# Low-rank mixing of an attention + mixer kernel: full sums of 32 rows and four row tiles at once, in two visits

## The chip, the cores and the metric

The kernel runs on one core of one Trainium2 chip. The metric is the device time of one execution in microseconds (us). Engines are named as the profile names them: PE (TensorE matmul), PEld (its weight load), DVE (VectorE), ACT (ScalarE), POOL (GpSimd), SP (SyncE, which issues most DMA). "Batch" is the index b from 0 to 7. Runs of one group were made on one chip beside runs of the kernel before on that chip; a ratio is the mean time of one kernel's fast runs over the mean of the other's fast runs of the same rounds, so it is not quite the ratio of the medians quoted beside it.

## The reference, cut to what matters

```python
# attention with RMS-normed q and k, 8 batches, 12 heads, 448 tokens, head size 64 -> x (8, 448, 768)
h   = x.transpose(0, 2, 1) @ U @ V          # low-rank token mixing: U 448x32, V 32x448
u   = x + h.transpose(0, 2, 1)
out = u + relu(u @ w_ch1) @ w_ch2           # channel MLP, 768 -> 3072 -> 768
```

In the layout of the kernel (tokens in partitions) the mixing of a batch is t = U^T x (32 x 768) and then u = x + V^T t. Tokens lie in four tiles of 128 rows.

## The kernel before

The main loop runs the MLP of batch b as a generator of short runs of matmuls. Between these runs it weaves first the attention of batch b+1 and then the mixing of batch b+1. The numbers `FA` and `FM` say which share of the MLP the attention and the mixing are spread over. Batch 0 is mixed otherwise and is not touched.

```python
FA, FM, NPE, FA0 = (0.74, 0.77), 0.09, 14, 0.66
...
def mix_t(b):                       # four partial sums, one per token tile, in four row groups of 32
    pm = ps_s.tile([P, 2, 512], FP32, tag="s", name="pm")
    for half in range(2):
        for i in range(4):
            nc.tensor.matmul(pm[i * rank:(i + 1) * rank, half, 0:HALF], Ub[:, b % 2, i, :],
                             xt[i][:, half * HALF:(half + 1) * HALF], start=True, stop=True)
    nc.scalar.activation(t4b.rearrange("p (h n) -> p h n", h=2), pm[:, :, 0:HALF], AF.Copy)

def mix_u(b, i, halves=(0, 1)):     # V stands four times in V4, so K=128 also adds the four partial sums
    pu = ps_s.tile([P, 2, 512], FP32, tag="s", name="pu") if b else ...
    for k, half in enumerate(halves):
        nc.tensor.matmul(pu[:, k, 0:HALF], lhsT, t4s[b][:, half * HALF:(half + 1) * HALF], start=True, stop=True)
    nc.vector.tensor_add(xv, pu[rows, 0:n, 0:HALF], xv)

def mix_uT(b, i):                   # u of the next first layer, transposed by DMA
    nc.sync.dma_start_transpose(us[b][:, :, i * P:(i + 1) * P], ...)

def mixing(b):
    items = [(1, lambda: mix_t(b))]
    for i in range(4):
        items.append((1, lambda i=i: (mix_u(b, i), mix_uT(b, i))))
    return items
...
def transposes(p):                  # q and k of a head pair; by DMA from batch 2 on (NPE = 14)
    if p < NPE: ...
    else:
        nc.sync.dma_start_transpose(qkT.rearrange("d s (j p) -> d (s j) p", j=NJ), qkn)

def gains(p):                       # the gain of q, on DVE, before the scores
    if p >= NPE:
        nc.vector.tensor_scalar(qkTs[p][:, 1], qkTs[p][:, 1], gg, None, OP.mult)
```

The score and mixing products share a pool of two PSUM tiles of two banks each (`ps_s`).

## Time and profile before

| | kernel before |
|---|---|
| time, median of 3 | 580.18 us (579.93 to 580.73) |
| PE busy | 562.7 of 579.7 us |
| product with V (`pu`), batches 1 to 7 | about 1.30 us each |
| x·U (`pm`), batches 1 to 7 | 0.44 us each |

The lines below are from the page of the kernel before: the span, the busy time of each engine with its share and count of instructions, the DMA queue that brings instructions (packets, MB, share of 16 engines' span), and the shares of the chain that ended last.

```profile
span 579.7 us, 11362 instructions
...
PE 562.7 (97%) x4613; PEld 306.5 (53%) x4613; DVE 397.8 (69%) x811; ACT 280.2 (48%) x413; POOL 78.3 (14%) x122
...
q8 instruction: 36, 0.59, 0.4%
...
PE 85%; DVE 7%; DMA 3%; ACT 2%; issue 1%; POOL 1%; DVEq 0%; POOLq 0%; ACTq 0%
```

TensorE is busy nearly all the time and makes up 85% of the chain, so time taken off TensorE should show nearly in full. Note the queue of 36 packets: 2 x 4613 TensorE instructions divided by 256 is 36.

The timeline of TensorE in the mixing of batch 7, kernel before. Columns: start in us, length in us (with the pipeline's tail), engine, line, operation, tiles, shapes, count.

```profile
505.57 0.34 PE L323 MATMUL pm<-xs,Ub 128*32 128x384 bf16 x1
505.57 0.34 PE L323 MATMUL pm<-x,Ub 128*32 128x384 bf16 x3
505.74 0.33 PE L323 MATMUL pm<-xs,Ub 128*32 128x384 bf16 x1
505.75 0.33 PE L323 MATMUL pm<-x,Ub 128*32 128x384 bf16 x3
506.01 1.15 PE L413 MATMUL pb<-Tw,hT 128*128 128x384 bf16 x6
507.00 0.49 PE L337 MATMUL pu<-t4b,Vsh 128*128 128x384 bf16 x2
507.32 1.14 PE L413 MATMUL pb<-Tw,hT 128*128 128x384 bf16 x6
508.30 0.49 PE L337 MATMUL pu<-t4b,V 128*128 128x384 bf16 x2
508.62 1.14 PE L413 MATMUL pa<-w2b,hT 128*128 128x384 bf16 x6
```

Four `pm` matmuls start together (505.57) and four more at 505.74; the next product starts at 506.01, so x·U takes 0.44 us. Each `pu` pair takes 0.32 us from its start to the next product's (507.00 to 507.32), and there are four.

The groups of TensorE by form, kernel before (count, then busy us and mean ns of one, then idle time before them and who ended it), show the row-tiled scores and the two mixing products:

```profile
L273 PE MATMUL sc<-qkT 64*128 64x448 bf16 x384 | 56.1, 358 | 3.3 <-ACT E L278 1.1 <-DVE qkT L265 0.8 <-DVE qkT L259 0.6
...
L337 PE MATMUL pu<-t4b,V 128*128 128x384 bf16 x48 | 12.1, 326 | 0.0
...
L323 PE MATMUL pm<-x,Ub 128*32 128x384 bf16 x42 | 3.5, 331 | 0.0
```

And in the waits of TensorE (who waited for whom: us in total, times, longest) the score line that matters later is small:

```profile
PE sc L273 <- DVE rec L302: 0.5, 1, 0.5
```

### The profile page before, as it was taken

The page shows a single profiled execution, that of the slowest core. Times are in us where ns is not written, and L with a number is a line of the kernel's source. Part 1 is how long each engine was busy: PE and PEld are TensorE (multiplying, and loading weights), DVE is VectorE, ACT ScalarE, POOL GpSimd, SP SyncE. Part 2 cuts the span into 40 slices and gives each one's busy share as a digit, 9 for nine tenths or more (in the row PEclk, how much of TensorE's full clock was granted, in tenths as well). Part 3 has the DMA queues.
Part 4 walks back from the last instruction along what each step waited for, and adds up shares of the span by engine and source line. Part 5 has one row for each costly group of instructions (what it writes and reads, how often), then busy time and mean ns, then how long its engine had stood idle before and what let it go on. Part 6 is the DMA issues. An engine that isn't in the chain of part 4 may idle for free.

```text
span 579.7 us, 11362 instructions
## 1 busy us (share of the span) xinstructions
PE 562.7 (97%) x4613; PEld 306.5 (53%) x4613; DVE 397.8 (69%) x811; ACT 280.2 (48%) x413; POOL 78.3 (14%) x122
## 2 busy tenths in 40 slices
PE   6799999999999999999999999999999999999997
PEld 2365556544565555544466555544456555554464
DVE  5868987399875787747777498747767487453342
ACT  5856663166621876166651677236661386302200
POOL 4651421000020001000020001000002010000010
PEclk9999999999999999999999999999999999999999
DMA  9999998415563355635536354546245441040021
GB/s 217 247 241 236 216 166 188 100 49 96 112 167 91 85 115 123 149 85 112 128 82 130 82 129 113 153 111 128 60 85 163 99 97 33 29 110 0 1 55 55
DMA packets 103648, 67.22 MB, mean 116 GB/s; under 512 B 54716, under 2 KB 102060, under 8 KB 103596
## 3 DMA queue, kind: packets, MB, share of 16 engines
q1 hardware_dynamic: 93988, 56.77, 42.0%
q0 software_dynamic: 9376, 9.44, 10.0%
q8 instruction: 36, 0.59, 0.4%
q10 hardware_dynamic: 232, 0.30, 0.2%
q14 instruction: 16, 0.13, 0.1%
HBM read 52.19 MB, written 11.01 MB: 109 GB/s over the span
## 4 chain that ended last, share of the span: by engine, by line
PE 85%; DVE 7%; DMA 3%; ACT 2%; issue 1%; POOL 1%; DVEq 0%; POOLq 0%; ACTq 0%
PE ph L488 35%; PE pb L413 10%; PE po L413 8%; PE o L299 7%; PE pe L413 7%; PE sc L273 7%; PE pa L413 6%; DMA qkT<-qkn 2%; DVE qkn L244 2%; ACT E L278 2%; PE pu L337 2%; PE warm L759 1%; DVE rstd L231 1%; PE first L732 1%; PE pt L257 1%
## 5 line engine op out<-in xcount | busy, mean ns | idle before, releaser
L488 PE MATMUL ph<-u,w1b 128*128 128x512 bf16 (+1 forms) x1128 | 232.8, 354 | 0.3
L278 ACT ACTIVATE E<-sc 112x896 bf16<-112x896 f32 x184 | 159.8, 914 | 59.3 <-PE sc L273 57.7
L488 PEld LDWEIGHTS <-w1b 128*128 128x128 bf16 x1128 | 102.8, 98 | 108.6 <-issue 22.5
L413 PEld LDWEIGHTS <-hT 128*128 128x128 bf16 x1080 | 101.3, 98 | 71.5 <-issue 8.8
L491 ACT ACTIVATE hT<-ph 128x384 bf16<-128x384 f32 (+1 forms) x95 | 51.4, 543 | 136.3 <-PE ph L488 134.4
L493 DVE TENSOR_SCALAR hT<-ph 128x512 bf16<-128x512 f32 (+1 forms) x93 | 57.9, 622 | 53.2 <-PE ph L488 52.4
L299 PEld LDWEIGHTS <-E 112*128 112x128 bf16 x1472 | 59.2, 99 | 16.5 <-DVE xs L306 1.8
L299 PE MATMUL o<-va,E 112*128 112x65 bf16 x1440 | 61.8, 195 | 0.7 <-DVE xs L306 0.7
L244 DVE TENSOR_TENSOR qkn<-qk,rstd 112x512 bf16<-112x512 f32 x84 | 56.5, 710 | 7.8 <-ACT rstd L237 3.9
L273 PE MATMUL sc<-qkT 64*128 64x448 bf16 x384 | 56.1, 358 | 3.3 <-ACT E L278 1.1
L720 POOL COPY scratch<-qkn 1x1 bf16<-1x1 bf16 x44 | 11.8, 268 | 309.7 <-DVE qkn L244 302.0
L413 PE MATMUL po<-w2b,hT 128*128 128x384 bf16 x288 | 52.5, 326 | 0.6 <-DVE hT L493 0.6
L231 DVE TENSOR_REDUCE rstd<-sq 112x16 f32<-112x1024 f32 x40 | 48.5, 1212 | 4.8 <-ACT sq L223 4.1
L413 PE MATMUL pa<-w2b,hT 128*128 128x384 bf16 x264 | 49.5, 326 | 0.0
L413 PE MATMUL pb<-Tw,hT 128*128 128x384 bf16 x264 | 48.0, 326 | 0.0
L223 ACT ACTIVATE sq<-qk 112x1024 f32<-112x1024 f32 x36 | 38.2, 1062 | 2.3 <-issue 1.1
L303 DVE TENSOR_TENSOR x<-o,rec 128x192 bf16<-128x192 f32 x96 | 34.3, 358 | 3.7
L448 POOL TENSOR_TENSOR o<-o,x 128x384 f32<-128x384 f32 x11 | 12.6, 1144 | 161.1 <-DVE o L447 161.1
L302 DVE RECIPROCAL rec<-o 128x4 f32<-128x4 f32 x96 | 17.0, 178 | 23.9 <-PE o L299 23.7
L273 PEld LDWEIGHTS <-qkT 64*128 64x128 bf16 x384 | 12.5, 94 | 35.6 <-issue 30.7
L428 ACT ACTIVATE pb<-pa 128x384 f32<-128x384 f32 x11 | 5.2, 475 | 50.3 <-PE pa L413 50.3
L339 DVE TENSOR_TENSOR x<-pu,x 128x768 bf16<-128x768 f32 (+1 forms) x27 | 23.3, 865 | 7.2 <-PE pu L337 7.0
(106 smaller groups left out, 449.7 us busy)
## 6 DMA issues: line engine op xcount, KB each, us to landing
qk<-in_k_dram SPq DMA_DIRECT2D x21, 448.0 KB, 6.1
vt<-in_v_dram SPq DMA_DIRECT2D x20, 448.0 KB, 5.0
qk<-in_q_dram SPq DMA_DIRECT2D x19, 448.0 KB, 3.7
w2b<-in_moe_w_ch_dram POOLq DMA_DIRECT2D x6, 768.0 KB, 9.7
w1b<-in_moe_w_ch_dram POOLq DMA_DIRECT2D x2, 1536.0 KB, 22.5
out_dram<-o SPq DMA_DIRECT2D x15, 168.0 KB, 2.7
out_dram<-o SPq DMA_DIRECT2D x16, 144.0 KB, 2.1
out_dram<-o SPq DMA_DIRECT2D x15, 120.0 KB, 2.5
```

The lines of the kernel that those rows point to most:

```text
L223: nc.scalar.activation(sqs[t, s][:, hs], qks[t, s][:, hs], AF.Square)
L231: nc.vector.tensor_reduce(rstds[t][:, s, hs].rearrange("p h j -> p (h j)"), sqs[t, s][:, hs].rearrange("p h (j d) -> p (h j) d", d=D), AX, ...
L244: nc.vector.tensor_tensor(qkn[:, s].rearrange("p j h d -> p h j d"), qks[t, s][:, hp].rearrange("p h (j d) -> p h j d", d=D), rstd[:, s, h ...
L273: nc.tensor.matmul(sc[:, hh, 0:S], kT[pp, kc * SP:kc * SP + P], qT[pp, :], start=True, stop=True)
L278: nc.scalar.activation(E_of(p)[:, :, PAD + kc * S:PAD + (kc + 1) * S], scs.pop((p, kc))[0:SP, :, 0:S], AF.Exp, scale=float(D) ** 0.5)
L299: nc.tensor.matmul(o[:, i, :], E[:, hh, c:c + P], va[:, hl, kc, :], start=(kc == 0), stop=(kc == NJ - 1))
L303: nc.vector.tensor_tensor(x3[:, :, d0:d0 + D], o[:, t0:t0 + 3, 0:D], rec[:, t0:t0 + 3].rearrange("p c -> p c ()").to_broadcast([P, 3, D]), ...
L339: nc.vector.tensor_add(xv, pu[rows, 0:n, 0:HALF], xv)
L413: nc.tensor.matmul(ps, lhs[:, c, :], rhs[:, c, :], start=first and c == 0, stop=last and c == NC - 1, skip_group_check=again)
L488: nc.tensor.matmul(ph, w1b[:, dc, hc * P:(hc + 1) * P], u[:, dc, :], start=(dc == 0), stop=(dc == KD - 1))
L491: nc.scalar.activation(hT[:, hc, 0:n], ph, AF.Relu)
L493: nc.vector.tensor_relu(hT[:, hc, 0:n], ph)
```

## The change

The intent is to cut the product with V by four in streamed columns. x·U now adds the four token tiles in PSUM (a full sum), with four blocks of 192 features in the four row groups, so that t has 32 rows per block. The product with V then runs with K=32 as four row tiles at once, each on its own PSUM bank. Two token tiles are done per visit, so two visits replace four. The shares of the weave are moved a little.

```diff
-    FA, FM, NPE, FA0 = (0.74, 0.77), 0.09, 14, 0.66
+    FA, FM, NPE, FA0 = (0.72, 0.75), 0.11, 14, 0.66
 ...
     def mix_t(b):
+        pm = ps_o.tile([P, BLK], FP32, tag="o", name="pm", padded_shape=[P, 4 * (D + 1)])   # BLK = 192
+        for i in range(4):
+            for j in range(4):
+                nc.tensor.matmul(pm[j * rank:(j + 1) * rank, :], Ub[:, b % 2, i, :],
+                                 xt[i][:, j * BLK:(j + 1) * BLK], start=(i == 0), stop=(i == 3))
+        nc.scalar.activation(t4b, pm, AF.Copy)
 ...
+    def mix_us(b, i0):
+        pus = [ps_s.tile([P, 2, 512], FP32, tag="s", name="pu") for _ in range(2)]
+        for k in range(2):
+            ...                          # off and edge: where V's columns of this token tile stand
+            for j in range(4):
+                r = slice(j * rank, (j + 1) * rank)
+                nc.tensor.matmul(pus[j // 2][:, j % 2, k * BLK:(k + 1) * BLK],
+                                 Vsh[r, par, :] if edge else V4[r, off:off + P], t4s[b][r, :], start=True, stop=True)
+        for k in range(2):
+            ...                          # rows and xv: the part of x that the sums are added to
+            for h in range(2):
+                nc.vector.tensor_add(xv, pus[h][rows, :, k * BLK:(k + 1) * BLK], xv)
+            mix_uT(b, i0 + k)
 ...
     def mixing(b):
-        items = [(1, lambda: mix_t(b))]
-        for i in range(4):
-            items.append((1, lambda i=i: (mix_u(b, i), mix_uT(b, i))))
+        items = [(.4, lambda: mix_t(b))]
+        for i in (0, 2):
+            items.append((1.2 + .4 * i, lambda i=i: mix_us(b, i)))
```

Per batch this is 32 matmuls instead of 16. With its weight load each matmul is two TensorE instructions, so a batch has 32 TensorE instructions more.

More of the change, by code (lines that the diff above doesn't have):

```diff
@@ L45 @@
     HALF = dm // 2
+    BLK = dm // 4
     PAD = 64
@@ L318, in mix_t @@
         xt = x_tiles(b)
-        t4b = upool.tile([P, dm], BF16, tag="t4b", name="t4b")
-        pm = ps_s.tile([P, 2, 512], FP32, tag="s", name="pm")
-        for half in range(2):
-            for i in range(4):
-                nc.tensor.matmul(pm[i * rank:(i + 1) * rank, half, 0:HALF], Ub[:, b % 2, i, :],
-                                 xt[i][:, half * HALF:(half + 1) * HALF], start=True, stop=True)
-        nc.scalar.activation(t4b.rearrange("p (h n) -> p h n", h=2), pm[:, :, 0:HALF], AF.Copy)
-        t4s[b] = t4b
+        t4b = upool.tile([P, BLK], BF16, tag="t4b", name="t4b", padded_shape=[P, dm])
+        pm = ps_o.tile([P, BLK], FP32, tag="o", name="pm", padded_shape=[P, 4 * (D + 1)])
[4 more added lines that the diff above has]
+        nc.scalar.activation(t4b, pm, AF.Copy)
+        t4s[b] = t4b
+    def mix_us(b, i0):
+        par = b % 2
+        pus = [ps_s.tile([P, 2, 512], FP32, tag="s", name="pu") for _ in range(2)]
+        for k in range(2):
+            off = OFFS[par][i0 + k]
+            edge = not 0 <= off < 384
+            for j in range(4):
[3 more added lines that the diff above has]
+        for k in range(2):
+            off = OFFS[par][i0 + k]
+            rows = slice(0, P) if 0 <= off < 384 else slice(64 * par, 64 * par + 64)
+            for h in range(2):
+                xv = x_tiles(b)[i0 + k][rows, h * HALF:(h + 1) * HALF].rearrange("p (j n) -> p j n", j=2)
+                nc.vector.tensor_add(xv, pus[h][rows, :, k * BLK:(k + 1) * BLK], xv)
+            mix_uT(b, i0 + k)
     def mix_u(b, i, halves=(0, 1)):
@@ L737, in mixing @@
     def mixing(b):
-        items = [(1, lambda: mix_t(b))]
-        for i in range(4):
-            items.append((1, lambda i=i: (mix_u(b, i), mix_uT(b, i))))
+        items = [(.4, lambda: mix_t(b))]
+        for i in (0, 2):
+            items.append((1.2 + .4 * i, lambda i=i: mix_us(b, i)))
         return items
```

## The prediction

> **What bounds the kernel.** TensorE. The page shows PE busy 562.7 of 579.7 us (97%); the chain of waits is 85% PE; DVE 69%, ACT 48%, granted clock full. PE time removed is worth nearly its full length, if no new PE wait replaces it.
>
> **What the change touches.** Only the mixing of batches 1 to 7. From the timeline of one (500 to 514 us):
> - x·U: eight 128x32 matmuls of 384 columns, first start 505.57, next product's start 506.01: 0.44 us. Four column tiles start together: already concurrent.
> - product with V: eight 128x128 matmuls of 384 columns in four pairs of 0.32 to 0.33 us: 1.30 us per batch, 9 us in all. The K=128 product adds four partial sums; a full sum needs 32 rows.
>
> **Removed.** The new product streams 4 rounds of 192 columns instead of 8 of 384, if four row tiles run at once. Scores (64-row pairs) show row tiles overlapping in this trace: four matmuls of 448 columns take 0.48 us (475.34 to 475.82), against 0.75 one after the other at the MLP's 0.163 us per 384 columns; that is 0.11 over pure overlap, for mode change and issue. The Trainium skill, "TensorE: Matmul & The Clock Gate", Part 3, gives 3.07x for four K=32 tiles at 512 columns. Estimate per visit: 2 x 0.08 + 0.11 to 0.19 = 0.27 to 0.35 us, two visits 0.55 to 0.7. Saved: 0.6 to 0.75 us per batch.
>
> **Added.** x·U has 16 matmuls for 8, same columns: 0 to 0.2 us per batch. The ACT copy of t4 falls from 0.81 to about 0.3 us (off the path). DVE adds go from 4 of 0.96 to 8 of about 0.55 us. Net PE gain: 0.4 to 0.7 us x 7 = 3 to 5 us.
>
> **Moved, and given back.** The visits come 2.0 (first), 2.9 or 3.9 us apart (12, 18, 24 matmuls); the second needs both score buffers back after four adds, 2.2 us: a few tenths lost once. More serious: in the mixings of batches 3, 5, 7 the second visit lies 36 matmuls (5.9 us) before the first layer, which needs all transposes of u. Its four adds queue on DVE behind the Strassen subtraction (0.96) and the o11 add (0.55), so the last transpose issues about 1.4 us later than before; it takes 2.8 to 3.4 us to land. The last such transition already waited about 0.2 us on it (chain: "DMA u<-x 3.40"). I expect 0.5 to 1 us of PE wait in each of the three, and 0.1 where the o22 add delays the reuse of pb: 1.5 to 3 us given back. After odd batches 48 matmuls follow; no wait. The shifted shares (0.74/0.77 to 0.72/0.75, 0.09 to 0.11) rearrange score and value pieces: +-1 us.
>
> **Prediction.** 580.2 - 4 + 2 = about 578 us, 574.8 to 581.6 in 8 of 10. Faster by over 2%: 0.01; within 2%: 0.97; slower: 0.02.
>
> **What would show it.** Right: pu matmuls of 32 rows starting four at a time, a visit of 0.27 to 0.4 us; pm stage 0.45 to 0.65 us; PE busy down 2 to 5 us; the first ph matmuls of batches 3, 5, 7 waiting for transposes of u. Wrong: visits over 0.6 us (row tiles serial or weight loads exposed); no wait at those transitions; new PE waits on scores or ACT in attention.
>
> **What would make it wrong.** Row tiles not overlapping (then slower by about 2 us); transposes landing with slack (about 576); the denser attention schedule stalling on ACT.

## The result

The changed kernel took 588.75 us (median of 6, 587.82 to 590.57) against 580.70 us (579.93 to 583.58). The ratio is 1.0129, with a 95% interval of 1.0098 to 1.0161. It is slower, and outside the predicted range. A later repeat (g1 below) gave 1.0122.

The same lines of the page, kernel after:

```profile
span 587.6 us, 11615 instructions
...
PE 561.9 (96%) x4725; PEld 304.8 (52%) x4725; DVE 395.5 (67%) x839; ACT 276.9 (47%) x413; POOL 77.3 (13%) x122
...
q8 instruction: 37, 0.61, 0.5%
...
PE 77%; DVE 10%; DMA 7%; ACT 3%; issue 1%; POOL 0%; SPq 0%; DVEq 0%; ACTq 0%
```

Busy time of PE fell by only 0.8 us, the span grew by 7.9 us, and in the chain the share of TensorE fell from 85% to 77% while DVE and DMA gained. The instruction queue carries one packet more.

Waits of TensorE, kernel after:

```profile
PE sc L274 <- DVE rec L303: 4.5, 3, 1.9
...
PE ph L508 <- DMA u<-x: 2.9, 3, 1.3
...
PE pm L324 <- DVE xs L307: 0.6, 3, 0.2
...
PE pm L324 <- DVE x L304: 0.5, 3, 0.2
```

The large ones are new: the scores wait 4.5 us in three places ("DVE rec" is only the last of several things waited for; the chain goes on to a DMA, shown below), and the first layer waits 2.9 us for the transposes of u.

Where the time went, by stage. A stage is the time from the first first-layer matmul of a batch to that of the next, read from the timelines of TensorE (us); the last column is the rest of the span.

| profile | head, b0 | b1 | b2 | b3 | b4 | b5 | b6 | b7 |
|---|---|---|---|---|---|---|---|---|
| before | 111.96 | 73.92 | 62.33 | 73.52 | 61.46 | 73.52 | 60.61 | 62.4 |
| after | 112.89 | 73.87 | 66.09 | 73.46 | 63.13 | 73.48 | 62.30 | 62.4 |
| e1 (old shares) | 111.80 | 73.41 | 64.24 | 72.99 | 65.23 | 73.03 | 61.68 | 62.4 |
| f3 (after + 128 instructions) | 109.35 | 73.87 | 62.26 | 73.46 | 61.45 | 73.48 | 61.29 | 62.4 |
| g4 (tuned) | 110.74 | 73.41 | 62.09 | 73.02 | 61.36 | 73.02 | 60.01 | 62.4 |

In the changed kernel the loss lies in batches 2, 4 and 6: +3.76, +1.67 and +1.69 us. The head varies by some us from profile to profile, the kernel before included (109.9 to 112.5 us in its profiles with other warm-ups, 111.96 here), so no cause is drawn from it.

**The row tiles work.** The timeline of a mixing in stage 1, kernel after:

```profile
171.49 0.26 PE L324 MATMUL pm<-x,Ub 128*32 128x192 bf16 x3
...
171.92 0.41 PE L324 MATMUL pm<-x,Ub 128*32 128x192 bf16 x9 [0.17 <-DVE x L304]
...
172.09 0.31 PE L324 MATMUL pm<-xs,Ub 128*32 128x192 bf16 x4
...
172.34 2.12 PE L433 MATMUL pa<-w2b,hT 128*128 128x384 bf16 x12
...
174.40 0.34 PE L338 MATMUL pu<-t4b,V 32*128 32x192 bf16 x8
...
174.67 2.12 PE L433 MATMUL pe<-Tw,S 128*128 128x384 bf16 x12
```

Eight row-tiled matmuls take 0.27 us until the next product starts (174.40 to 174.67), against 0.65 us for the two pairs they replace. Here x·U took 0.85 us instead of 0.44 (171.49 to 172.34): it starts 6 matmuls after the last values and waits for their normalization on DVE.

**The last transposes of u are late.** The timeline at the end of batch 6, kernel after:

```profile
517.58 0.34 PE L338 MATMUL pu<-t4b,V 32*128 32x192 bf16 x8
517.69 0.96 DVE L460 TENSOR_TENSOR hT<-hT 128x1536 bf16<-128x1536 bf16 x1 [0.47 <-PE pa L433]
...
518.57 0.55 DVE L462 TENSOR_TENSOR o<-pa,x 128x384 f32<-128x384 f32 x1
519.03 1.94 DVE L345 TENSOR_TENSOR x<-pu,x 128x384 bf16<-128x384 f32 x4
...
525.22 1.04 PE L508 MATMUL ph<-u,w1b 128*128 128x512 bf16 x4 [1.34 <-DMA u<-x]
```

The second visit's four adds start on DVE only after the subtraction and the o11 add, at 519.03, and the first layer of batch 7 waits 1.34 us. This is the wait that was predicted, in its place; f3 below shows that the late visit makes only about 0.3 us of it.

**The transposes of q and k are late, which was not predicted.** First the issue of one DMA transpose on SP's queue, then what came of it on DVE and PE in batch 2. Kernel before:

```profile
201.15 1.22 SPq L261 DMA_TRANSPOSE qkT<-qkn  x1
```

```profile
207.98 0.34 DVE L265 TENSOR_SCALAR qkT<-qkT,gg 128x448 bf16<-128x448 bf16 x1 [1.33 <-DMA qkT<-qkn]
...
208.47 0.56 PE L273 MATMUL sc<-qkT 64*128 64x448 bf16 x4 [0.47 <-DVE rec L302]
```

The same two views of the kernel after:

```profile
201.79 1.22 SPq L262 DMA_TRANSPOSE qkT<-qkn  x1
```

```profile
207.49 1.14 PE L508 MATMUL ph<-u,w1b 128*128 128x384 bf16 x6
...
210.06 0.34 DVE L266 TENSOR_SCALAR qkT<-qkT,gg 128x448 bf16<-128x448 bf16 x1 [2.78 <-DMA qkT<-qkn]
...
210.55 0.56 PE L274 MATMUL sc<-qkT 64*128 64x448 bf16 x4 [1.92 <-DVE rec L303]
...
211.04 3.68 PE L508 MATMUL ph<-u,w1b 128*128 128x384 bf16 x12
```

The program order around is the same, and the three loads of 448 KB ahead of the transpose have the same spacing. From the issue to the gain on DVE it took 6.83 us before and 8.27 us after, and the score wait grew from 0.47 to 1.92 us. Then the 12 first-layer matmuls behind the wait took 3.68 us. They take 2.12 elsewhere. The view of windows of the kernel after tells why; its columns are the window, its length, the busy time of PE, PEld, DVE, ACT and POOL, then the granted clock, DMA share and GB/s:

```profile
211.50:214.50 3.00, 3.00 (x11) 1.32 (x9) 2.35 (x5) 2.61 (x4) 0.18 (x1) 0.50 0.26 50
214.90:218.00 3.10, 3.10 (x39) 1.76 (x37) 2.81 (x8) 1.66 (x3) 0.36 (x2) 1.00 0.01 2
```

The granted clock was half (0.50) for 3.4 us after that wait. Half the work of 3.4 us is lost, so about 1.7 us by estimate. In the profiles waits of 1.85, 1.92, 2.06 and 2.65 us in mid-kernel were followed by such a stretch, and waits of 1.80, 1.75 and 1.73 us were not. The six runs of the changed kernel tell the half clock from the rest: three had a granted clock of 0.990 to 0.994 and took 589.4 to 590.6 us, three had 1.000 and took 587.8 to 588.1. So half-clock stretches cost about 2 us in the runs that have them, and without any the kernel is still over 1% slower.

**What held the transpose up.** The DMA records of the trace hold one more thing at that moment. The DMA view of the kernel after, 207.8 to 209.1 us (queue: packets, MB, share):

```profile
q1 hardware_dynamic: 162, 0.03, 12.6%
q8 instruction: 1, 0.02, 5.0%
```

One packet of 16 KB from the instruction queue started at 207.93 us and took 1.05 us on its DMA engine. By 208.63 us, 15 of the 16 completions of the transpose had come. The 4-byte write of the last one ran at 208.97, the moment at which the instruction packet ended, and the completion was seen at 210.04. In the kernel before, such a packet ran at 207.29 for 1.07 us, just when the transpose's packets on all engines were done; all 16 completions came within 0.24 us.

The packets of this queue come once per 256 TensorE instructions. The Trainium skill, "Runtime: NRT & Kernel Launch", section "Instruction fetch mechanics", states that a sequencer refills its instruction memory in 16 KiB blocks of 256 instructions over its own DMA queue, and calls the cost "mostly hidden". Size and interval agree with this trace: 36 packets for 9226 instructions before, 37 for 9450 after. The 32 instructions that each mixing adds move the fetches against the program, by 64 instructions in batch 2, 128 in batch 4 and 192 in batch 6.

### The profile page after: what moved, and what is told of

It reads as the page before. It is cut to its first block, busy times and chain, and to the rows that moved or that the text cites. A ratio compares the mean times of both kernels' runs of the same rounds, so it can differ in the third digit from the quotient of the medians.

```text
span 587.6 us, 11615 instructions
## 1 busy us (share of the span) xinstructions
PE 561.9 (96%) x4725; PEld 304.8 (52%) x4725; DVE 395.5 (67%) x839; ACT 276.9 (47%) x413; POOL 77.3 (13%) x122
## 4 chain that ended last, share of the span: by engine, by line
PE 77%; DVE 10%; DMA 7%; ACT 3%; issue 1%; POOL 0%; SPq 0%; DVEq 0%; ACTq 0%
PE ph L508 32%; PE pb L433 8%; PE pa L433 8%; PE po L433 8%; PE sc L274 7%; PE o L300 6%; PE pe L433 6%; DMA qkT<-qkn 4%; ACT E L279 2%; DVE qkn L245 2%; DMA u<-x 2%; DMA qk<-in_k_dram 1%; DVE x L304 1%; DVE rstd L232 1%; DVE hT L424 1%
## 5 line engine op out<-in xcount | busy, mean ns | idle before, releaser
L740 POOL COPY scratch<-qkn 1x1 bf16<-1x1 bf16 x44 | 9.0, 205 | 307.9 <-DVE qkn L245 301.7
L433 PE MATMUL pa<-w2b,hT 128*128 128x384 bf16 x264 | 47.1, 326 | 0.0
L433 PE MATMUL pe<-Tw,S 128*128 128x384 bf16 x132 | 24.3, 327 | 0.0
L433 PE MATMUL pb<-w2b,hT 128*128 128x384 bf16 x132 | 23.8, 326 | 0.0
```

Of the source, the lines that this page charges most:

```text
L433: nc.tensor.matmul(ps, lhs[:, c, :], rhs[:, c, :], start=first and c == 0, stop=last and c == NC - 1, skip_group_check=again)
```

## The experiments

Theories: (A) the squeezed attention share makes the scores wait; (B) the new mixing pieces as such cost the time; and, after the first group, (C) the shifted instruction fetches do.

### e1: the changed pieces with the shares of before

```diff
-    FA, FM, NPE, FA0 = (0.72, 0.75), 0.11, 14, 0.66     # on the changed kernel
+    FA, FM, NPE, FA0 = (0.74, 0.77), 0.09, 14, 0.66
```

> The changed kernel with the woven shares of the kernel before (0.74/0.77 and 0.09), the two-visit mixing kept. Theory A (the squeezed attention share makes scores wait for the transposes of q and k in batches 2, 4, 6): those waits fall back to under 1.5 us in all, the time falls to about 582, and only the waits for the transposes of u (about 3 us) stay. Theory B (the mixing pieces themselves cost the time: two visits, late transposes of u, wait of x*U for the last values): the time stays at 586 to 588.

Measured: 586.66 us, ratio 1.0087 (1.0057 to 1.0117). The score waits of 1.5 us and more stayed (1.52 and 2.06 us in batches 2 and 4), so A falls as the main cause; the time is in the range that B gave. In the odd stages the gain now shows: 73.41 against 73.92 us.

### e2: the shares alone, on the kernel before

```diff
-    FA, FM, NPE, FA0 = (0.74, 0.77), 0.09, 14, 0.66     # on the kernel before
+    FA, FM, NPE, FA0 = (0.72, 0.75), 0.11, 14, 0.66
```

> The kernel before with only the shares of the change (0.72/0.75 and 0.11); its mixing pieces are untouched. Theory A: 584 to 586 us, with score waits of 3 to 5 us in batches 2, 4, 6. Theory B: within 1 us of the kernel before, 580 to 581.

Measured: 582.57 us, ratio 1.0012 (0.9969 to 1.0054). Not distinguishable from the kernel before, and the interval leaves out the 1.3% of the changed kernel. Its waits of the scores on "DVE rec" add up to 2.4 us against 0.5 before, fewer than the 3 to 5 us that A gave. So the shares may cost a little here, but they are not the main cause.

### e3: the last visit earlier

```diff
-    FA, FM, NPE, FA0 = (0.72, 0.75), 0.11, 14, 0.66     # on the changed kernel
+    FA, FM, NPE, FA0 = (0.74, 0.77), 0.06, 14, 0.66
```

> As e1, but the mixing share is 0.06, so the last visit lies 48 matmuls instead of 36 before the first layer of batches 3, 5, 7, two microseconds earlier. If the waits of the first layer for the transposes of u come from the late second visit, they vanish (0 instead of about 3 us); but the visits are then only 6 matmuls apart in those batches, so the second waits 1 to 1.3 us for its score buffers in each. Total about 1 us below e1 to equal. If the transposes are late for another reason (the queue), the waits stay.

Measured: 584.52 us, ratio 1.0037 (0.9993 to 1.0081). Waits of TensorE in e3:

```profile
PE sc L274 <- DVE qkT L266: 3.9, 6, 1.9
...
PE pu L338 <- DVE x L345: 3.7, 8, 0.9
```

The wait of the first layer for u is gone from the list, so an earlier last visit is enough to hide it. In its place the visits wait for their PSUM tiles, 3.7 us in all. The score waits are still there.

### e4: four visits with row tiles

```diff
-        for i in (0, 2):
-            items.append((1.2 + .4 * i, lambda i=i: mix_us(b, i)))
+        for i in range(4):                 # mix_us takes one token tile: four matmuls, two adds; mix_t's weight is 1
+            items.append((1, lambda i=i: mix_us(b, i)))
-    FA, FM, NPE, FA0 = (0.72, 0.75), 0.11, 14, 0.66
+    FA, FM, NPE, FA0 = (0.74, 0.77), 0.09, 14, 0.66
```

> As e1, but one token tile in each of four visits, with the weights of the kernel before: four row tiles, one round of 192 columns. Each visit should take 0.18 to 0.2 us against 0.325 in the kernel before, the adds of one tile (1.1 us) lie between visits 1 us apart, so 0.1 to 0.5 us wait for buffers at each later visit. Waits for the transposes of u as in the kernel before. If the row tiles are a gain and grouping is what costs, this is 577 to 581; if the full sums themselves cost, it stays over 584.

Measured: 591.83 us, ratio 1.0173 (1.0136 to 1.0210): a miss, slower than anything expected. Each visit took 0.19 us as expected, but the six matmuls before it took 1.08 us instead of 0.97, read here as about 0.1 us for entering the row-tiled mode, and a round of visit and six matmuls took 1.27 us (452.68 to 453.95 in the profile) against 1.30 before. Nothing is left of the gain: the odd stages are 73.92 to 74.34 us. Grouping two tiles per visit is therefore needed. In the even stages the same score waits appear (1.73 and 1.48 us).

All four kernels with the new pieces have these waits, and they have in common 32 more TensorE instructions per batch. That led to theory C.

### f1: the kernel before with the instruction count of the changed one

```diff
+                cut = b > 0 and hc < 4 and 0 < dc < KD - 1
+                for c in ((slice(0, 256), slice(256, n)) if cut else (slice(0, n),)):
-                nc.tensor.matmul(ph, w1b[...], u[:, dc, :], ...)
+                    nc.tensor.matmul(ph[:, c], w1b[...], u[:, dc, c], ...)
```

> The kernel before, its mixing and shares untouched; only 16 first-layer matmuls in each of batches 1 to 7 are split in two by columns, so TensorE has 32 instructions more per batch, at the start of the stage, and its instruction count at every later point is that of the changed kernel. Same arithmetic. Theory C (TensorE fetches its instructions in 16 KB blocks, one per 256 instructions[...]; 32 more per batch move a fetch into the moment when the transposes of q and k are due): scores wait 1.5 us or more in batch 2 and about 2 us in batch 4, as in the changed kernel and e1, e3, e4; total 583 to 585. Rival (the row-tiled pieces or their SBUF and PSUM traffic cause the late transposes): waits as in the kernel before (0.5 and 0), total 580 to 582.

Measured: 583.04 us, ratio 1.0022 (0.9999 to 1.0045). The time lies at the lower edge of what theory C gave, but only 1.3 us or so were lost, and the waits are those of the rival: no score wait of 1.5 us appears. In its profile the fetch in batch 2 ran 5.8 us after the issue of the transpose, much as in the changed kernel, and yet the transpose was not held up. A fetch in the wait is not enough; see the table below and what follows it.

### f2, f3, f4: the changed kernel with 64, 128 and 192 more TensorE instructions in the head

```diff
-        heat(NWARM)              # 16 warm-up matmuls of 512 columns
+        heat(NWARM + 32, 170)    # f2; f3: heat(NWARM + 64, 102); f4: heat(NWARM + 96, 73)
...                              # heat gets a second argument, the columns of a matmul; about 8192 columns in all stay
```

> The changed kernel with its 16 warm-up matmuls of 512 columns cut into 48 of 170: 64 more TensorE instructions in the head, nothing else. Theory C: the fetches move by 64 instructions (about 5 us) against the program in all batches, so the score waits of batches 2 and 4 (1.92, 0.81, 1.75 us) change, vanish or appear elsewhere; the time moves by over 1 us. The waits for the transposes of u (0.9, 0.65, 1.3) stay in every case, as the late second visit causes them. Rival: score waits as in the changed kernel, 588.

> As f2 with 128 more instructions. Theory C: another set of score waits; at least one of the three paddings under 586. Rival: 588 in all three.

> As f2 with 192 more instructions; with the 64 that the mixings of batches 1 and 2 add, batch 2 has the fetch phase of the kernel before (256 is one block). Theory C: in batch 2 the score wait falls from 1.9 to about 0.5 us. Rival: it stays near 1.9.

Measured: f2 584.25 us, 1.0044 (1.0021 to 1.0066); f3 580.82 us, 0.9990 (0.9955 to 1.0025); f4 581.81 us, 1.0016 (0.9983 to 1.0050). Nothing but the warm-up was touched, and up to 8 us went. Waits of TensorE in f3:

```profile
PE sc L274 <- DVE rec L303: 1.6, 3, 0.9
...
PE ph L508 <- DMA u<-x: 0.9, 3, 0.3
```

In f4 the score wait of batch 2 fell to 0.46 us, as expected from the fetch phase of the kernel before.

I had expected the waits for u to stay in every case. They fell as well, from 2.9 us (0.90, 0.65 and 1.34) to 0.9 us, about 0.3 us each, in f3 and in f4. So the late visit makes 0.3 us of each wait; the rest goes with the phase. For the last of them the traces show it: the last transpose of u took 3.79 us to land in the changed kernel, with a fetch in between, and 2.77 us in f3, without one.

### g1, g2, g3: repeat and controls

g1 is the changed kernel unedited. g2 adds a whole block of 256 instructions, so the head is that of f2 to f4 in kind while the phase behind it is unchanged. g3 does the same to the kernel before.

```diff
-        heat(NWARM)
+        heat(NWARM + 128, 56)    # g2 on the changed kernel, g3 on the kernel before
```

> The changed kernel once more, unedited, beside its control on one chip. If the loss is the kernel's and not that of a chip or a day: 587 to 590 us, score waits of 1.5 us and more in batches 2 and 4.

> Control for f2 to f4: the warm-up cut into 144 matmuls of 56 columns, so 256 more TensorE instructions, one whole fetch block: the head changes as in f2 to f4, the fetch phase of everything behind it does not. Theory C (phase): span behind the head as in g1, with its score waits; only the head is 2 to 3 us shorter, total about 585. Rival (the shorter head or the moved start heals it, not the phase): as f3 and f4, 580 to 582.

> The kernel before with the same cut warm-up, same phase. Tells what the head alone is worth: if f2 to f4 owed 2 to 3 us to it, this is 577 to 579; if nothing, 580 to 582. No new score waits.

Measured: g1 588.94 us, 1.0122 (1.0084 to 1.0159); g2 590.29 us, 1.0141 (1.0106 to 1.0176); g3 581.57 us, 1.0007 (0.9962 to 1.0052). Waits of TensorE in g2:

```profile
PE sc L274 <- DVE rec L303: 4.5, 3, 2.7
...
PE ph L508 <- DMA u<-x: 3.8, 3, 1.6
```

With one whole block added, the loss is all there; g2 was expected somewhat shorter, as I had thought the head would gain, and it does not. So what healed f3 and f4 is the phase in the block of 256 instructions, not the shorter warm-ups.

### h1, h2: the kernel before with 64 and 128 more instructions

```diff
-        heat(NWARM)              # on the kernel before
+        heat(NWARM + 32, 170)    # h1; h2: heat(NWARM + 64, 102)
```

> The kernel before with 64 more TensorE instructions in the warm-up, mixing untouched. If the fetch phase alone makes the score waits, batch 2 (where the changed kernel is 64 instructions ahead) now waits about 1.5 us and the time is 582 to 585; if the old mixing is not sensitive to the phase, as f1 hints, 580 to 582.

> The kernel before with 128 more, the padding of g4. If g4 owes its gain to the phase alone, this too is 577 to 578; if the gain is the row-tiled mixing's, this stays at 580 to 583.

Measured: h1 582.82 us, 1.0057 (1.0003 to 1.0110); h2 585.70 us, 1.0096 (1.0050 to 1.0141). TensorE in h1 at the same place of batch 2:

```profile
204.73 1.14 PE L488 MATMUL ph<-u,w1b 128*128 128x384 bf16 x6
207.44 0.56 PE L273 MATMUL sc<-qkT 64*128 64x448 bf16 x4 [1.57 <-DVE rec L302]
```

The old mixing is sensitive too: 64 warm-up instructions more give it a score wait of 1.57 us, and 128 make it 1% slower, with not one number of its arithmetic changed. h2 was slower than I expected (580 to 583).

### g4, h3: a version that beats both, with and without padding

```diff
-    FA, FM, NPE, FA0 = (0.72, 0.75), 0.11, 14, 0.66     # on the changed kernel
+    FA, FM, NPE, FA0 = (0.74, 0.77), 0.08, 14, 0.66     # g4 and h3
-        heat(NWARM)
+        heat(NWARM + 64, 102)                           # g4 only
```

> A candidate to beat both: the changed mixing with the shares 0.74/0.77 and a mixing share of 0.08, which puts the last visit of batches 3, 5, 7 at 42 matmuls (not 36) before the first layer and keeps 12 between the visits, and the warm-up padding of f3 (128 instructions). Waits for u at most 0.3 us in all but the last, for the score buffers about 0.3 us each; score waits depend on the phase. 575 to 579 us.

> g4 without its padding: the fetch phase of the changed kernel. If the phase costs what f2 to f4 and g2 say, the score waits of batches 2 and 4 come back (1.5 us and more each) and the time is 582 to 586; if the shares and the place of the last visit did it, 577 to 579.

Measured: g4 577.59 us (576.09 to 578.10, 6 runs), 0.9926 (0.9897 to 0.9955), faster than both kernels. h3 580.42 us, 1.0008 (0.9962 to 1.0054). Waits of TensorE in g4:

```profile
PE sc L274 <- DVE qkT L266: 0.9, 4, 0.3
...
PE sc L274 <- DVE rec L303: 0.4, 1, 0.4
```

No wait for u is left, the odd stages have the gain of e1, and the score waits are those of the kernel before. h3 shows what the padding does: without it the wait of 1.61 us in batch 4 is back. But h3 missed its expectation of 582 to 586 us, and it changes the reading: it has the instruction count of the changed kernel and no padding, and differs from e1 in the mixing share alone (0.08 for 0.09, the last visit 6 matmuls earlier), which takes the ratio from 1.0087 to 1.0008. In its profile no wait for u is left, and the transpose of batch 2 took 6.72 us with a fetch at +6.0, so that it was not held up. The padding is one cure and not the only one.

### The transposes and the fetches in all profiles

Of the transposes of q and k that directly follow three loads of 448 KB, about ten in a profile, the table has the two at which the scores of the changed kernel waited longest: the time from issue to the gain on DVE, and the start (and length) of the 16 KB instruction packet nearest to it, counted from the issue of the transpose. All are from the DMA records and the timelines, in us; "early" (it started over 3 us before the issue) and "none" mean that none ran between the issue and the gain.

| profile | batch 2: transpose | fetch | batch 4: transpose | fetch |
|---|---|---|---|---|
| before | 6.83 | +6.1 (1.07) | 6.69 | early |
| e2 | 6.53 | +5.8 (1.05) | 7.42 | early |
| g3 (before + 256) | 6.66 | +5.9 (1.09) | 7.14 | early |
| f1 (before, split) | 6.44 | +5.8 (0.97) | 6.40 | +5.6 (1.10) |
| h1 (before + 64) | 7.92 | +5.8 (1.10) | 6.76 | none |
| h2 (before + 128) | 7.47 | +3.0 (1.33) | 6.77 | +6.0 (1.09) |
| after | 8.27 | +6.1 (1.05) | 7.78 | +3.7 (2.40) |
| g1 (after again) | 8.10 | +5.8 (0.95) | 7.95 | +5.5 (1.09) |
| g2 (after + 256) | 6.52 | +5.8 (1.08) | 8.81 | +6.0 (1.64) |
| e1 | 7.87 | +5.8 (1.00) | 8.77 | +3.9 (2.64) |
| e3 | 8.09 | +6.0 (1.11) | 8.98 | +6.1 (1.64) |
| e4 | 8.08 | +6.0 (1.12) | 8.60 | +3.4 (2.92) |
| h3 | 6.72 | +6.0 (1.08) | 8.74 | +6.0 (1.69) |
| f2 (after + 64) | 7.34 | +2.8 (1.33) | 6.98 | -0.3 (1.17) |
| f3 (after + 128) | 6.65 | early | 6.57 | early |
| f4 (after + 192) | 6.81 | +6.0 (1.06) | 7.05 | +5.7 (1.68) |
| g4 | 6.75 | early | 7.05 | early |

Every transpose of this table over 7.45 us (14 of 34) has a fetch between its issue and its end. Without one in between the times are 6.57 to 7.42 us. With one they are 6.40 to 8.98 us.

The kept traces hold a wider test: the same transposes in all 17 profiles, with the fetches at other places. Taken are the transposes whose landing (the last of 16 completions) the trace tells.

- Transposes of u issued after 170 us: the 239 without a fetch between issue and landing took 2.72 to 2.95 us. Of the 53 with one, 34 took 3.06 to 4.81 us. Where the fetch ended after the landing (14), none took over 2.88 us; where it ended before the landing, 34 of 39 were late.
- Transposes of q and k, each against the median of the same transpose without a fetch: 6 of 257 without a fetch are over 0.4 us late, and 56 of 120 with one.
- The transposes of batch 2 in the table with a fetch at +5.8 to +6.1: in the six long ones (after, g1, e1, e3, e4, h1) a last 4-byte write ran within 0.2 us of the fetch's end. In the seven short ones (before, e2, g3, f1, g2, h3, f4) all these writes had run by 0.13 us after the fetch's start.

So in batch 2 a fetch at the same distance delays the transpose where a write of the transpose still comes after it, and not where all have run before.

## Why the prediction was wrong

The time was predicted at 578.0 us (574.8 to 581.6) and came out at 588.75.

1. **Right: TensorE bounds the kernel, and the row tiles overlap.** The Trainium skill, "TensorE: Matmul & The Clock Gate", Part 3, gives 3.07x for four K=32 tiles at 512 columns; here, at 192 columns, two visits of 0.27 us replace 1.30 us, a factor of 2.4. With about 0.1 us more for entering the mode (12 matmuls before a visit take 2.06 us in e1, 448.18 to 450.24, where 12 take 1.95 elsewhere), the saving is 0.5 us per batch, and e1 shows it in each odd stage (73.92 to 73.41). The prediction said 0.4 to 0.7.
2. **Off in size: the net PE gain in the changed kernel itself.** Its odd stages gained only 0.05 us. In the one shown, x·U took 0.85 us instead of the predicted 0.45 to 0.65, because it waits for the last values. Its new place in the weave does that, which the prediction did not cost.
3. **Right in place, in size by luck: the waits for u.** Predicted were 0.5 to 1 us in each of three, 1.5 to 3 us in all; measured were 0.90, 0.65 and 1.34. e3 took them away by moving the visit, which hides both parts. But in f3 and f4, with the visits in the same place, they were 0.28 to 0.31 us each, 0.9 us in all. The queue on DVE, which the prediction reasoned from, is worth that much; the other 2 us go with the phase.
4. **The step that failed: "PE time removed is worth nearly its full length, if no new PE wait replaces it", with the new waits listed as u alone and the rest set at "+-1 us" for the shares.** The shares were worth nothing that e2 could tell. A term was missing: 224 more TensorE instructions. In the profile of the changed kernel the score waits of batches 2 and 4 grew from 0.47 to 1.92, 0.81 and 1.75 us, so by 4.0 us, and the half clock behind the first added about 1.6 us (3.68 against 2.12 us for the same 12 matmuls). With the phase moved (f3) the changed kernel was level with the kernel before (0.9990) and not the 2 us faster that were forecast: points 2 and 3 and score waits of 1.6 us (0.5 before) stand against the gain.

What is shown: shifting the TensorE instruction count by 128 or 192, and nothing else behind the head, removes the loss; shifting it by 256 does not; the kernel before becomes 1% slower with a shift of 128. The same transposes land on time without an instruction fetch in between and are often late with one, and in batch 2 the late ones are those with writes left when the fetch ends. What stays open: why, with a fetch at nearly the same distance, a write stands behind it in one profile (8.27 us at +6.1) and not in another (6.83 at +6.1), and so why f1 lost only 1.3 us. The records do not name the DMA engine of a packet, so that the two share one is argued. That the fetches cause all of the loss, in the runs whose traces were not kept too, is likewise inferred: h2, for instance, lost more than the waits in its one profile add up to, and h3 lost nothing at the phase of the changed kernel.

## What to carry to other kernels

The time of this kernel, TensorE-bound with DMA transposes just in time, depended on where in a block of 256 instructions the program stood. In such a kernel, before judging a change of 1%, pad both versions by a few instruction counts that are no multiple of 256 and compare them at their best (here 577.6 against 580.0 to 581.8 us for the unpadded kernel before, whose paddings of 64 and 128 were worse; 192 was not tried on it). Count instructions as a cost of finer tiling, beside columns. A late visit is late for the DMA behind it as well: place the last write of a tensor by the engine queue that it joins, not by the matmul it follows.

## What the Trainium skill lacked or had wrong

- "Runtime: NRT & Kernel Launch", "Instruction fetch mechanics", calls the refill "mostly hidden". Block size and interval are as it says (37 packets of 16 KB for 9450 TensorE instructions), but here each packet took 0.9 to 2.9 us, and transposes were late behind it: those of the table took up to 8.98 us with a fetch inside and 6.57 to 7.42 us without, and the phase of the fetches moved whole kernels by 1% and more (588.9 and 590.3 us at shifts of 0 and 256; 584.3, 580.8 and 581.8 at 64, 128 and 192).
- No page says that adding instructions anywhere earlier, warm-up included, can change the time of a later stage: h2, 128 warm-up instructions, 580.0 to 585.7 us.
- "TensorE: Matmul & The Clock Gate", "Why this matters for your kernels", advises no idle gaps over about 3 us. Here a gap of 1.85 us was already followed by a half clock for 3.4 us, while one of 1.80 us was not.
- No page gives a time for entering and leaving the row-tiled mode within other work, and the same page's model for packing, Part 3, has no term for it. Here it is about 0.1 us before each visit (six matmuls take 1.08 instead of 0.97 us in e4), enough to cancel the gain of a visit with a single round of four tiles.
